# First block with a shared value tile, a late mirror and one home for the stage-1 table

## The chip, the cores and the metric

The kernel runs on one core of one Trainium2 chip. The metric is the device time of one launch in microseconds (us), taken as the median of three runs; less is better. TensorE is the matmul engine (PE in the profile, its weight loads PEld), DVE is VectorE, ACT is ScalarE, POOL is GpSimd, SP is SyncE, which here only issues DMAs.

## The reference

Two layers, one after the other. The first takes the real part of a two-dimensional Fourier transform of each batch, over 3008 rows and 256 columns. The second is a gated feed-forward layer on its result.

```python
X = np.fft.fft(np.fft.fft(x, axis=1), axis=2).real     # x: 8 x 3008 x 256, float32
t = X.reshape(24064, 256)
out = (np.maximum(t @ w_gate, 0) * (t @ w_val)) @ w_out  # w_gate, w_val: 256 x 1536, w_out: 1536 x 256
```

## The kernel before, in words

The row transform is factored as 94 x 32. Stage 1 (`stage1`, and `first_products` for batch 0) multiplies the input rows with a 94-point table of cosines and sines, a shuffle through memory turns the result, and stage 2 finishes the row transform with a small table `m2`. Its result per batch is three blocks of 512 columns, each held as a pair of bf16 tiles `pq` (pool `pqp`, five buffers). The column transform over 256 is not computed on the data: it is folded into the weights by `fold_w` with a table of cosines and sines, `cd` (the "D table"), at the start.

Because the input is real, each computed column gives two output rows, a direct one and a mirrored one. The feed-forward layer walks 288 steps t, 12 per block (`NF` = 12 slices of 128 of the hidden width). For a step, `gate(t)` (L615) puts the direct gate into one bank of PSUM, G, with two matmuls; ACT takes its relu as gs (L621); `mirror_gate(t)` (L623) adds a third matmul to the same G and ACT takes that relu as gm (L628). So the third matmul must wait until ACT has read G for gs. `value(t, 0)` and `value(t, 1)` (L630, matmul L634, weights wc and ws) put the direct value into V; `value(t, 2)` (weights wm) adds the mirror part on top. `direct_h` (L644) is a DVE product of gs and V, `mirror_h` (L650) of gm and the mirrored V. `out_piece` (L667) multiplies the products of the block before with `w_out`.

There are two forms of the loop. The first block (t = 0 to 11, loop at L790) has no output work yet. There the mirror value is made by the third matmul, which overwrites the direct value in place: `value(t, 2)` has to come after `direct_h(t)` has read V, and `mirror_h(t)` comes after it on DVE. A step writes, in the order of TensorE's queue: mirror gate of t-1, two gate matmuls of t, the mirror value of t-1, two value matmuls of t, then what `between(t)` hands in. From t = 12 on (loop at L804) the steps run in pairs, the mirror value is worked out on DVE and POOL (`even`, `mirror_value`), V of two steps is one tile of two banks, and out pieces are woven in.

The order of the work is written out by hand: every engine takes its instructions in the order of the program text, and a framework adds the semaphores that the tiles' reads and writes need. `between(t)` runs what the table `extra` holds for step t: in the first block the rest of the weight fold (`fold_w`, L329, two fp32 matmuls, an ACT copy and for the sine half a DVE product `scale_w`), of the stage between the two transforms (`upright`, `rotate`) and of stage 2; from t = 12 on, stage 1 of the next batch. `pace` hands POOL its share of folding the next batch's input.

`pair(t, name)` (L598) gives the tile that two steps t, t+1 share, each with its half. In the first block V is the exception: L601 to L605 give each step a whole two-bank tile of its own, of which it uses one half. The pool `psv` has two such buffers.

At the start (L348 to L570) ACT and DVE make the tables while the first batch arrives by DMA. `wn` (two signs of the stage-1 table) lies in the pool `sp`, which is given up after the start; `w1`, a copy of one half of it made by two ACT copies (L467, L530), stays for the later batches. The D table's three ACT instructions are L511 to L513. The read of `t1t` at L516 (`seen`) is a small DMA that SP issues when the ACT copy `first_evac(4)` (L515, code at L230) is done; eight weight loads and the first load of batch 1 stand behind it on SP.

Of the kernel before, what the change touches and what calls it, by code (L numbers as in the profile page):

```python
# [11 lines left out]
F32 = mybir.dt.float32  # L12
BF16 = mybir.dt.bfloat16
# [3 lines left out]
SB = bass.MemoryType.SB  # L17
# [27 lines left out]
def kernel(ctx: ExitStack, tc, x, w_gate, w_val, w_out, out):  # L45
# [3 lines left out]
    nc = tc.nc  # L49
    B, S, D = x.shape  # L50
    DF = w_gate.shape[1]
    NA, NB = 94, 32
    H = D // 2
    NF = DF // 128
# [5 lines left out]
    const = ctx.enter_context(tc.tile_pool(name="const", bufs=1, space=SB))  # L60
# [3 lines left out]
    psg = ctx.enter_context(tc.tile_pool(name="psg", bufs=2, space=PS))  # L64
    psv = ctx.enter_context(tc.tile_pool(name="psv", bufs=2, space=PS))
    pso = ctx.enter_context(tc.tile_pool(name="pso", bufs=1, space=PS))
    pqp = ctx.enter_context(tc.tile_pool(name="pqp", bufs=5, space=SB))

    ctx.enter_context(tc.manual_schedule())

# [64 lines left out]
                in_offset=bass.IndirectOffsetOnAxis(ap=ixf[:, k:k + 1], axis=0))  # L135

    turn = {"o": 0, "v": 0}

    def spare(name):

        turn["o"] += 1
        return pso.tile([128, 512], F32, tag=f"o{turn['o'] % 2}", name=name)

    def borrow(name):

        return pso.tile([128, 512], F32, tag=f"o{(turn['o'] + 1) % 2}", name=name)
# [8 lines left out]
    def stage1(b, c, evac):  # L155

        ps, eo = borrow("ps1"), xt[b]["eo"]
        for i in range(2):
            jj = 2 * c + i
            o = ps[0:96, i * D:(i + 1) * D]  # L160
            if jj:
                nc.tensor.matmul(o, lhsT=w1[:, jj, :], rhs=eo[:, jj, :], start=True, stop=True)  # L162
                continue
            for cs, lo, hi in ((0, 0, H + 1), (1, H + 1, D)):
                for k in range(2):
                    nc.tensor.matmul(ps[0:96, lo:hi], lhsT=wz[:, cs, k, :], rhs=eo[:, k * (J - 1), lo:hi],  # L166
                                     start=(k == 0), stop=(k == 1))
        evacuate(b, c, ps, evac)
# [9 lines left out]
        else:  # L178
            nc.vector.tensor_copy(dst, src)

    psf, tabs = {}, {}

    def ends(r, n):

# [99 lines left out]


    ix = const.tile([96, 2, B], I32, tag="ix")
    w1 = const.tile([NA, 16, 96], BF16, tag="w1")
    wz = const.tile([NA, 3, 2, 96], BF16, tag="wz")
    m2 = const.tile([128, 2, 128], BF16, tag="m2")
    rot = const.tile([128, 128], BF16, tag="rot")  # L290
# [13 lines left out]
    for n in range(DF // 512):  # L304
        for c in range(3):
            pair = hp.tile([128, 2, 512], F32, tag="h", name="wst")
            for i in range(2):
                wst[i, n, c] = pair[:, i, :]
    cd = hp.tile([128, 2, 512], F32, tag="h", name="cd")[:, :, 0:H]
# [38 lines left out]
    with tc.tile_pool(name="sp", bufs=1, space=SB) as sp:  # L348
        dve, pl = nc.vector, nc.gpsimd

        def residue(t, q, n, eng):

            eng.tensor_scalar(q, t, scalar1=1.0 / n, scalar2=RND, op0=ALU.mult, op1=ALU.add)
            eng.tensor_scalar(q, q, scalar1=-RND, scalar2=float(n), op0=ALU.add, op1=ALU.mult)
            eng.tensor_tensor(t, t, q, op=ALU.subtract)

        def sines(out, r, n, sign):
            nc.scalar.activation(out, r, ACTF.Sin, scale=sign * 2.0 * math.pi / n * (1.0 - 2e-7))

        def cosines(out, a, n):  # L360

            nc.scalar.activation(out, a, ACTF.Sin, scale=-2.0 * math.pi / n, bias=qpi[0:a.shape[0], :])

        def absolute(out, a):
            nc.scalar.activation(out, a, ACTF.Abs)
# [1 line left out]
        def iota(eng, out, pattern, base, mult):  # L367
            eng.iota(out, pattern=pattern, base=base, channel_multiplier=mult, allow_small_or_imprecise_dtypes=True)

        wn = tabs["wn"] = sp.tile([NA, 2, 16, 96], BF16, tag="wn", name="wn")  # L370
        tabs["wzn"] = sp.tile([NA, 2, 96], BF16, tag="wzn", name="wzn")
        tabs["back"] = sp.tile([NA, NB, H], BF16, tag="back", name="back")
        ixf = sp.tile([96, 3], I32, tag="ixf")
# [6 lines left out]
        da = sp.tile([128, H], F32, tag="da")  # L380
        dq = sp.tile([128, H], F32, tag="dq")
# [52 lines left out]
        def bits(shift, mask):  # L434
            ti = sp.tile([128, 1], I32, tag=f"b{shift}{mask}i")
            dve.tensor_scalar(ti[:], pi[:], scalar1=shift, scalar2=mask,
                              op0=ALU.logical_shift_right, op1=ALU.bitwise_and)
            tf = sp.tile([128, 1], F32, tag=f"b{shift}{mask}f")
            dve.tensor_copy(tf[:], ti[:])
            return tf  # L440
# [23 lines left out]
        for k in range(2):  # L464
            sines(free(wz[:], 192 * (k + 1), [97, 2], [2, 48]), both[0], S, 2.0 * k - 1.0)
        nc.scalar.mul(wn[:, 0, 9:16, :], wn[:, 1, 9:16, :], -1.0)
        nc.scalar.copy(w1[:, 1:10, :], wn[:, 1, 1:10, :])  # L467
        back(0, 2, "dve")
        dve.tensor_scalar(da[:], dd[:], scalar1=mi[:], scalar2=None, op0=ALU.mult)
        residue(da[:], dq[:], D, dve)  # L470
        jj, sl, up, odd = bits(0, 15), bits(4, 1), bits(5, 3), bits(0, 1)

        ends(24, 8)
# [34 lines left out]
        ends(16, 4)  # L508
        back(16, 4, "dve")
        dve.tensor_scalar(tis[:], tis[:], scalar1=NB - 1, scalar2=None, op0=ALU.bitwise_and)  # L510
        absolute(dq[:], da[:])  # L511
        cosines(cd[:, 0, 1:H], dq[:, 1:H], D)
        sines(cd[:, 1, 1:H], da[:, 1:H], D, 1.0)  # L513
        group((6, 7, 0), False)
        first_evac(4, "act")  # L515
        nc.sync.dma_start(out=seen[:], in_=t1t[0][0:1, 0, 8:10])  # L516
# [10 lines left out]
        first_evac(0, "dve")  # L527
        for cs in range(2):
            dve.tensor_tensor(m2[:, cs, :].rearrange("p (u k) -> p u k", u=4), sv[cs][:], ui[:], op=ALU.mult)
        nc.scalar.copy(w1[:, 10:16, :], wn[:, 1, 10:16, :])  # L530

        iota(pl, di[:], [[-32, 4], [-16, 2], [-1, 16]], 0, 1)
        pl.tensor_scalar(s2[:], mi[:], scalar1=1.0, scalar2=-2.0, op0=ALU.min, op1=ALU.mult)
# [60 lines left out]
    def split(t):  # L594

        return t >= NF

    def pair(t, name):  # L598

        e = pairs.setdefault(t // 2, {})  # L600
        if name == "V" and not split(t):  # L601
            name = f"V{t % 2}"
            if name not in e:
                e[name] = psv.tile([128, 2, 512], F32, tag="v", name="V")
            return e[name]  # L605
        if name not in e:
            pool, shape, dt = {"h": (hp, [128, 2, 2, 512], BF16), "gs": (gp, [128, 2, 512], F32),
                               "V": (psv, [128, 2, 512], F32), "gm": (ep, [128, 2, 512], F32),
                               "E": (ep, [128, 2, 512], F32)}[name]
            e[name] = pool.tile(shape, dt, tag=name.lower(), name=name)  # L610
        return e[name]
# [3 lines left out]
    def gate(t):  # L615
        b, blk, f = steps[t]
        pq, fs, ds = pqt[b, blk], slice(f * 128, (f + 1) * 128), direct(t)
        G = Gt[t] = psg.tile([128, 512], F32, tag="g", name="G")
        nc.tensor.matmul(G[:, ds], lhsT=wc[0][:, fs], rhs=pq[:, 0, ds], start=True, stop=False)  # L619
        nc.tensor.matmul(G[:, ds], lhsT=ws[0][:, fs], rhs=pq[:, 1, ds], start=False, stop=True)  # L620
        nc.scalar.activation(pair(t, "gs")[:, t % 2, ds], G[:, ds], ACTF.Relu)  # L621
# [8 lines left out]
    def value(t, k):  # L630
        b, blk, f = steps[t]
        cs = mirrored(t) if k == 2 else direct(t)
        w = (wc, ws, wm)[k][1]
        nc.tensor.matmul(pair(t, "V")[:, t % 2, cs], lhsT=w[:, f * 128:(f + 1) * 128],  # L634
                         rhs=pqt[b, blk][:, min(k, 1), cs], start=(k == 0), stop=(k > 0 or split(t)),
                         skip_group_check=(k == 2 or k == 1 and split(t)))
# [7 lines left out]
    def direct_h(t, n):  # L644

        ds, k = direct(t), slice(t % 2, t % 2 + n)
        nc.vector.tensor_tensor(pair(t, "h")[:, k, 0, 0:ds.stop - ds.start], pair(t, "gs")[:, k, ds],  # L647
                                pair(t, "V")[:, k, ds], op=ALU.mult)

    def mirror_h(t, n, eng, val):  # L650

        cols, k = mirrored(t), slice(t % 2, t % 2 + n)
        w = cols.stop - cols.start
        eng.tensor_tensor(free(pair(t, "h")[:], 1024 * (t % 2) + 512 + w - 1, [1024, n], [-1, w]),  # L654
                          pair(t, "gm")[:, k, cols], val[:, k, cols], op=ALU.mult)
# [89 lines left out]
    for n in (1, 2):  # L745
        t = 4 * n
# [36 lines left out]
    n = len(steps) // 2  # L783

    def between(t):
        for fn in extra.get(t, ()):
            fn()
        pace(t)

    for t in range(NF + 1):  # L790
        if t:
            mirror_gate(t - 1)
        if t < NF:
            gate(t)
        if t:
            value(t - 1, 2)
            mirror_h(t - 1, 1, nc.vector, pair(t - 1, "V"))
        if t < NF:
            value(t, 0)
            value(t, 1)  # L800
            direct_h(t, 1)
            between(t)

    for p in range(NF // 2, n + NF // 2):  # L804
        t = 2 * p
        live = p < n
        if NF // 2 < p <= n:
            mirror_gate(t - 1)
        if live:
            value(t, 0)  # L810
            value(t + 1, 0)
            gate(t)
        out_piece(t - NF, 0)
        between(t)
        if NF // 2 < p <= n:
            direct_h(t - 2, 2)
        if live:
            even(t)
            even(t + 1)
        out_piece(t - NF, 1)  # L820
        if live:
            mirror_gate(t)
            gate(t + 1)
        out_piece(t + 1 - NF, 0)
        between(t + 1)
        if NF // 2 < p <= n:
            mirror_value(p - 1)
        if live:
            value(t, 1)
            value(t + 1, 1)  # L830
        out_piece(t + 1 - NF, 1)
# [30 lines left out]
```

## Time and profile before

| what | value |
|---|---|
| median of 3 runs | 625.57 us (625.12 to 625.66) |
| the profiled execution's own time | 625.63 us |
| its span in the trace | 623.9 us |
| TensorE busy, share of the span | 612.0 us, 98% |
| DVE busy | 536.7 us, 86% |
| ACT busy | 445.5 us, 71% |
| POOL busy | 520.0 us, 83% |
| mean granted TensorE clock | 0.997 |

The profile describes one execution. Its times in us count from the start of the span, which is 1.7 us shorter than the time of that execution. A row of the timeline gives the start, the duration, the engine, the line, the operation with output and inputs, and in brackets how long the engine was idle ahead of it and who ended that. A matmul is shown from its start to the modelled end of its pipeline, so that matmuls in a dense stream overlap: with 496 columns one takes 0.37 us, and the next starts 0.21 us after it. Whether TensorE lost time is read from the distance between starts, not from the busy share.

### The profile page before, as it was taken

How to read it: one execution, taken by the hardware profiler on the slowest of the kernel's cores; microseconds unless marked ns; L12 is line 12 of the kernel's file. 1: busy time of each engine (PE TensorE's matmuls, PEld its weight loads, DVE VectorE, ACT ScalarE, POOL GpSimd, SP SyncE). 2: the span in 40 equal slices, each digit the busy share in tenths (PEclk: the TensorE clock that was granted, in tenths of full speed). 3: DMA queues.
4: the chain of work that ended last, by engine and by line, in shares of the span. 5: the costliest groups of instructions: out<-in, count | busy, mean ns of one | idle time of the engine just before them, and what ended most of it. 6: DMA issues, size and time to landing. Idle time of an engine off the chain costs nothing.

```text
span 623.9 us, 11929 instructions
## 1 busy us (share of the span) xinstructions
PE 612.0 (98%) x4252; PEld 409.3 (66%) x4284; DVE 536.7 (86%) x652; ACT 445.5 (71%) x857; POOL 520.0 (83%) x447
## 2 busy tenths in 40 slices
PE   8999999999999999999999999999999999999996
PEld 4345666766666666666667666666666666666665
DVE  7677898899889898888988998898988888899991
ACT  7676777777776767767677767767677776766660
POOL 8898898999888898899988998888988965565664
PEclk9999999999999999999999999999999999999998
DMA  8994282525553182613833255531822134112114
GB/s 168 240 169 109 82 219 67 134 65 163 125 136 79 34 234 71 164 36 86 222 100 92 63 162 127 134 82 34 230 72 61 34 85 125 52 34 67 34 35 99
DMA packets 42038, 67.44 MB, mean 108 GB/s; under 512 B 5877, under 2 KB 31774, under 8 KB 39962
## 3 DMA queue, kind: packets, MB, share of 16 engines
q1 hardware_dynamic: 37162, 50.61, 31.4%
q0 software_dynamic: 4656, 15.88, 10.7%
q8 instruction: 33, 0.54, 0.4%
q10 hardware_dynamic: 160, 0.20, 0.1%
q14 instruction: 27, 0.22, 0.1%
HBM read 38.85 MB, written 30.17 MB: 111 GB/s over the span
## 4 chain that ended last, share of the span: by engine, by line
PE 96%; DMA 1%; POOL 1%; issue 1%; DVE 1%; ACT 0%; POOLq 0%; DVEq 0%
PE po L683 40%; PE V L634 19%; PE G L619 10%; PE G L626 10%; PE G L620 10%; PE psw L333 2%; PE ps L162 2%; PE ps L271 2%; DMA lo<-in_x_dram 1%; POOL hi L132 0%; DVE h L647 0%; PE pst L240 0%; PE ps L216 0%; PE ps L166 0%; POOL lo L129 0%
## 5 line engine op out<-in xcount | busy, mean ns | idle before, releaser
L654 POOL TENSOR_TENSOR h<-gm,E 128x992 bf16<-128x992 f32 (+1 forms) x138 | 319.9, 2318 | 83.3 <-DVE E L661 54.4
L683 PE MATMUL po<-wo,h 128*128 128x256 bf16 (+2 forms) x2304 | 328.5, 272 | 0.4
L683 PEld LDWEIGHTS <-h 128*128 128x128 bf16 (+2 forms) x2304 | 231.4, 103 | 105.9
L628 ACT ACTIVATE gm<-G 128x496 f32<-128x496 f32 (+1 forms) x288 | 170.4, 592 | 94.7 <-PE G L626 87.7
L647 DVE TENSOR_TENSOR h<-gs,V 128x1024 bf16<-128x1024 f32 (+3 forms) x150 | 173.8, 1159 | 59.4 <-PE V L634 39.3
L641 DVE SCALAR_TENSOR_TENSOR E<-nb,af,V 128x496 f32<-128x496 bf16 (+1 forms) x276 | 190.2, 731 | 0.4 <-PE G L620 0.4
L621 ACT ACTIVATE gs<-G 128x497 f32<-128x497 f32 (+2 forms) x288 | 169.7, 589 | 25.3 <-PE G L620 25.2
L661 DVE SCALAR_TENSOR_TENSOR E<-E,V 128x992 f32<-128x992 f32 (+1 forms) x138 | 164.6, 1193 | 0.0
L619 PE MATMUL G<-pq,wc 128*128 128x496 bf16 (+2 forms) x287 | 107.6, 375 | 1.2
L620 PE MATMUL G<-pq,ws 128*128 128x497 bf16 (+2 forms) x288 | 108.0, 375 | 0.1
L626 PE MATMUL G<-pq,wm 128*128 128x496 bf16 (+1 forms) x288 | 107.9, 375 | 0.0
L634 PE MATMUL V<-pq,ws 128*128 128x496 bf16 (+2 forms) x280 | 83.7, 374 | 0.0
L634 PE MATMUL V<-pq,wc 128*128 128x496 bf16 (+2 forms) x266 | 80.7, 374 | 0.0
L620 PEld LDWEIGHTS <-ws 128*128 128x128 bf16 x288 | 28.2, 98 | 32.6
L696 ACT COPY os<-po 128x512 f32<-128x512 f32 x63 | 36.9, 586 | 14.3 <-PE po L683 11.7
L634 PEld LDWEIGHTS <-wc 128*128 128x128 bf16 x288 | 28.2, 98 | 20.7 <-issue 2.5
L114 POOL TENSOR_TENSOR eo<-xla 94x256 bf16<-94x256 f32 x56 | 40.5, 729 | 0.6
L619 PEld LDWEIGHTS <-wc 128*128 128x128 bf16 x288 | 28.2, 98 | 18.5 <-DVE pq L278 0.8
L114 POOL TENSOR_TENSOR eo<-xlb 94x256 bf16<-94x256 f32 (+1 forms) x42 | 34.4, 820 | 0.7
L111 POOL TENSOR_TENSOR xla<-xla,xha 94x510 f32<-94x510 f32 x28 | 32.9, 1175 | 2.2
L177 ACT CAST t<-ps 96x512 bf16<-96x512 f32 x56 | 32.7, 584 | 2.3 <-PE ps L162 0.2
L626 PEld LDWEIGHTS <-wm 128*128 128x128 bf16 x288 | 28.1, 98 | 4.4 <-issue 1.6
(142 smaller groups left out, 367.8 us busy)
## 6 DMA issues: line engine op xcount, KB each, us to landing
out_dram<-os SPq DMA_DIRECT2D x124, 128.0 KB
Td<-t SPq DMA_DIRECT2D x7, 768.0 KB
t<-Td SPq DMA_DIRECT2D x7, 768.0 KB
out_dram<-os SPq DMA_DIRECT2D x82, 64.0 KB
xla<-in_x_dram SPq DMA_DIRECT2D x7, 720.0 KB
xlb<-in_x_dram SPq DMA_DIRECT2D x6, 640.0 KB
nb<-Nd SPq DMA_DIRECT2D x23, 128.0 KB
out_dram<-os SPq DMA_DIRECT2D x40, 48.0 KB
```

The source lines that it names most:

```text
L114: yield eng.tensor_tensor(e1[:, :, k:k + H], x1[:, :, 0:H], free(x1, D, [DX, n], [-1, H]), op=op)
L619: nc.tensor.matmul(G[:, ds], lhsT=wc[0][:, fs], rhs=pq[:, 0, ds], start=True, stop=False)
L620: nc.tensor.matmul(G[:, ds], lhsT=ws[0][:, fs], rhs=pq[:, 1, ds], start=False, stop=True)
L621: nc.scalar.activation(pair(t, "gs")[:, t % 2, ds], G[:, ds], ACTF.Relu)
L626: nc.tensor.matmul(G[:, cols], lhsT=wm[0][:, f * 128:(f + 1) * 128], rhs=pqt[b, blk][:, 1, cols], start=False, stop=True, skip_group_check ...
L628: nc.scalar.activation(pair(t, "gm")[:, t % 2, cols], G[:, cols], ACTF.Relu)
L634: nc.tensor.matmul(pair(t, "V")[:, t % 2, cs], lhsT=w[:, f * 128:(f + 1) * 128], rhs=pqt[b, blk][:, min(k, 1), cs], start=(k == 0), stop=( ...
L641: nc.vector.scalar_tensor_tensor(pair(t, "E")[:, t % 2, cols], nbt[b, blk][:, cols], af[:, f:f + 1], pair(t, "V")[:, t % 2, cols], op0=ALU ...
L647: nc.vector.tensor_tensor(pair(t, "h")[:, k, 0, 0:ds.stop - ds.start], pair(t, "gs")[:, k, ds], pair(t, "V")[:, k, ds], op=ALU.mult)
L654: eng.tensor_tensor(free(pair(t, "h")[:], 1024 * (t % 2) + 512 + w - 1, [1024, n], [-1, w]), pair(t, "gm")[:, k, cols], val[:, k, cols], o ...
L661: nc.vector.scalar_tensor_tensor(E[:, :, cols], E[:, :, cols], 2.0, V[:, :, cols], op0=ALU.mult, op1=ALU.subtract)
L683: nc.tensor.matmul(po[0:m, i, :], lhsT=pair(t - f + ff, "h")[:, ff % 2, sg, g * 128:g * 128 + m], rhs=wo[:, ff, :], start=(ff == 0), stop= ...
```

## The change

In the first block V goes by `pair` like everything else: steps t and t+1 share one tile of two banks. The mirror value and its product move behind the direct work of the next step: the step now writes mirror gate of t-1, gate of t, value of t, `direct_h(t)`, then `value(t-1, 2)` and `mirror_h(t-1)`, then `between(t)`. The last mirror of the block goes into the first pair of the second loop, behind `gate(12)`. `wn` moves to the pool `const`, `w1` and its two copies go, and stage 1 of the later batches reads `wn`. One of the five buffers of `pqp` goes. The three ACT instructions of the D table move from behind `back(16, 4)` to right behind the DVE work that they read.

```diff
-    pqp = ctx.enter_context(tc.tile_pool(name="pqp", bufs=5, space=SB))
+    pqp = ctx.enter_context(tc.tile_pool(name="pqp", bufs=4, space=SB))
...
-                nc.tensor.matmul(o, lhsT=w1[:, jj, :], rhs=eo[:, jj, :], start=True, stop=True)
+                nc.tensor.matmul(o, lhsT=wn[:, 1, jj, :], rhs=eo[:, jj, :], start=True, stop=True)
...
-    w1 = const.tile([NA, 16, 96], BF16, tag="w1")
+    wn = tabs["wn"] = const.tile([NA, 2, 16, 96], BF16, tag="wn", name="wn")
...
-        wn = tabs["wn"] = sp.tile([NA, 2, 16, 96], BF16, tag="wn", name="wn")
...
         nc.scalar.mul(wn[:, 0, 9:16, :], wn[:, 1, 9:16, :], -1.0)
-        nc.scalar.copy(w1[:, 1:10, :], wn[:, 1, 1:10, :])
         back(0, 2, "dve")
         dve.tensor_scalar(da[:], dd[:], scalar1=mi[:], scalar2=None, op0=ALU.mult)
         residue(da[:], dq[:], D, dve)
+        absolute(dq[:], da[:])
+        cosines(cd[:, 0, 1:H], dq[:, 1:H], D)
+        sines(cd[:, 1, 1:H], da[:, 1:H], D, 1.0)
...
-        absolute(dq[:], da[:])
-        cosines(cd[:, 0, 1:H], dq[:, 1:H], D)
-        sines(cd[:, 1, 1:H], da[:, 1:H], D, 1.0)
         group((6, 7, 0), False)
         first_evac(4, "act")
...
-        nc.scalar.copy(w1[:, 10:16, :], wn[:, 1, 10:16, :])
...
         e = pairs.setdefault(t // 2, {})
-        if name == "V" and not split(t):
-            name = f"V{t % 2}"
-            if name not in e:
-                e[name] = psv.tile([128, 2, 512], F32, tag="v", name="V")
-            return e[name]
...
-    for t in range(NF + 1):
+    def last_value(t):
+
+        value(t, 2)
+        mirror_h(t, 1, nc.vector, pair(t, "V"))
+
+    for t in range(NF):
         if t:
             mirror_gate(t - 1)
-        if t < NF:
-            gate(t)
+        gate(t)
+        value(t, 0)
+        value(t, 1)
+        direct_h(t, 1)
         if t:
-            value(t - 1, 2)
-            mirror_h(t - 1, 1, nc.vector, pair(t - 1, "V"))
-        if t < NF:
-            value(t, 0)
-            value(t, 1)
-            direct_h(t, 1)
-            between(t)
+            last_value(t - 1)
+        between(t)
 
     for p in range(NF // 2, n + NF // 2):
         t = 2 * p
         live = p < n
-        if NF // 2 < p <= n:
+        if p <= n:
             mirror_gate(t - 1)
         if live:
             value(t, 0)
             value(t + 1, 0)
             gate(t)
+        if p == NF // 2:
+            last_value(t - 1)
```

More of the change, by code (lines that the diff above doesn't have):

```diff
@@ L137 @@
     turn = {"o": 0, "v": 0}
+    tabs = {}
     def spare(name):
@@ L179, in evacuate @@
             nc.vector.tensor_copy(dst, src)
-    psf, tabs = {}, {}
+    psf = {}
     def ends(r, n):
```

## The prediction, made before the result was known

> **What bounds the kernel now.** First the waits of TensorE, over the whole span (engine and line, whom it waited for: us in total, times, longest):
>
> ```profile
> PE V L634 <- DVE h L647: 1.4, 3, 0.8
> ...
> PE ps L216 <- ACT t L230: 0.4, 1, 0.4
> PE psw L333 <- DVE wm L327: 0.2, 1, 0.2
> ```
>
> TensorE is 98% busy; taking the distances between matmul starts against their dense spacing, I find no lost time after 51.4 us that isn't a missing record. So only a shift of the first 52 us can move the end, and whatever moves there moves it one for one. The waits on `direct_h` (L647) are the target of the late mirror, the wait at L216 that of the D table. Second, the timeline of TensorE at the end of the first block:
>
> ```profile
> 46.15 0.37 PE L626 MATMUL G<-pq,wm 128*128 128x496 bf16 x1
> ...
> 47.18 0.37 PE L634 MATMUL V<-pq,wm 128*128 128x496 bf16 x1 [0.24 <-DVE h L647]
> ...
> 48.96 0.37 PE L634 MATMUL V<-pq,wm 128*128 128x496 bf16 x1 [0.36 <-DVE h L647]
> ...
> 49.58 0.37 PE L626 MATMUL G<-pq,wm 128*128 128x496 bf16 x1
> 50.74 0.37 PE L634 MATMUL V<-pq,wm 128*128 128x496 bf16 x1 [0.79 <-DVE h L647]
> ```
>
> The mirror matmul (wm) of V comes late because it overwrites what `direct_h` reads. Six matmuls need 6 x 0.21 = 1.25 us; these steps take 1.5 to 1.8. Third, ACT and DVE there:
>
> ```profile
> 46.55 0.58 ACT L628 ACTIVATE gm<-G 128x496 f32<-128x496 f32 x1 [0.46 <-PE G L626]
> 47.03 0.58 ACT L621 ACTIVATE gs<-G 128x496 f32<-128x496 f32 x1
> ...
> 48.69 0.58 ACT L621 ACTIVATE gs<-G 128x496 f32<-128x496 f32 x1
> ```
>
> ```profile
> 48.24 0.66 DVE L647 TENSOR_TENSOR h<-gs,V 128x496 bf16<-128x496 f32 x1
> ```
>
> A mirror gate at time 0 gives gm at 0.41 and gs at 0.88 to 1.46, and the next mirror gate may start at 1.52: a loop through ACT that stays after the change. Also to be seen: gs of step 11 starts at 48.69 in one half of the tile whose other half the product that began at 48.24 still reads (0.66 us, to 48.90). Halves of an SBUF tile are kept apart. Fourth, the second loop, where V already is one tile of two steps:
>
> ```profile
> 108.44 0.58 PE L634 MATMUL V<-pq,wc 128*128 128x496 bf16 x2
> ...
> 109.19 1.37 DVE L641 SCALAR_TENSOR_TENSOR E<-nb,af,V 128x496 f32<-128x496 bf16 x2
> ```
>
> The two matmuls write the two halves and end at 108.81 and 109.02. The first `even` reads only the first half. Yet in the trace's semaphore records the first matmul raises no semaphore, the second does, and DVE's queue passes its wait for TensorE at 109.06, 0.04 after the second end. The same 0.04 comes back in many other pairs. In the other direction too: of two `even`s only the second raises a semaphore, and of the two wc/ws matmul pairs only the first waits. **In PSUM the halves of a V tile count as one tile.**
>
> **What the skill says.** "PSUM — Partial Sum Buffer", section "PSUM bank collisions raise a hardware error": two engines may use different banks at once. The trace agrees: at 45.87 to 46.54 `mirror_h` reads one V buffer while TensorE writes another from 45.81. So the chip asks for no wait between halves; it is the program's semaphores. "TensorE: Matmul & The Clock Gate", "Back-to-back issue gap": N/2.4 + 2.5 ns, 209 ns for 496 columns; the trace has 0.21. Its section "What's actually happening": the clock falls after an idle window of about 3.4 us. Gaps of 1.0 us in this trace left the granted clock at 0.997, and mine below are up to 1.4, so I add nothing. "ScalarE: Activation LUTs", "Table sets": functions of one set need no reload; the trace has one table load, though sines and copies alternate, so moving the D table adds none.
>
> **The change, part by part.**
>
> *The D table and the two copies.* ACT at 8.20 gets three instructions (0.93 us from first start to end at 13.34) where the first copy of `w1` (0.89) goes; ACT then idles until 9.80 (DMA), so nothing behind it moves. At 13.34 they go, and `first_evac(4)` starts when its matmuls end (13.79 + 0.04) instead of 14.18. TensorE, waiting at 14.71, starts 0.36 sooner. What is late next: the first `fold_w` at 16.62 needs the DVE difference L323, which waits for weights that land at 15.2, and ends at 16.63; its second half loads at 16.68 in either case. So at most 0.05 is left; I take 0. SP passes the wait at `seen` 0.36 sooner, with ten DMAs behind it; the DMA engines are idle from 15.2 to 16.8, so nothing is pushed aside. If that cover went, the gain would be 0.36. The second copy (0.67 at 17.14) ends as ACT's next input arrives: 0.
>
> *One home, four buffers.* Stage 1 reads equal values with equal loads: 0. A `pqp` buffer is written again four blocks on instead of five. Stage 2 of the next batch comes at steps 29 to 37 of a batch, and the block four places back was finished at steps 0, 12 and 24, at least 10 steps (some 20 us) before: 0. If wrong, a wait of a step, 2 us, per batch; I see no way to it.
>
> *The late mirror.* No instruction is added. `value(t-1, 2)` moves behind two value matmuls, its product behind `direct_h(t)`. Behind the waiting matmul stand all of `between(t)` and the next step, since TensorE works in order. Two cases by the parity of t:
>
> - t even: the mirror goes to the older pair, whose `direct_h` is long done. No wait; the old ones go.
> - t odd: t-1 and t share a tile. `direct_h(t)`, written just before, reads it. The mirror of t-1 writes the other half, and by the fourth view must wait for the end of `direct_h(t)`: that is for gs(t), 0.06 to the start, 0.67 for the product, 0.05 to TensorE.
>
> Price of the odd steps, from this trace: the slot of the moved matmul is where the sixth matmul of the step stands now, and gs(t) ends where it does now.
>
> | t | gs(t) ends | wait over at (+0.78) | slot | stall |
> |---|---|---|---|---|
> | 1 | 25.75 | 26.52 | 25.12 | 1.40 |
> | 3 | 30.80 | 31.57 | 30.38 | 1.19 |
> | 5 | 36.03 | 36.80 | 35.61 | 1.19 |
> | 7 | 41.49 | 42.26 | 41.07 | 1.19 |
>
> Together 4.97. TensorE is dense there except for 0.2 at 38.78, whose chain (fold, ACT, `scale_w`) moves along with it, so nothing is absorbed. Steps 9 to 12 (times without these 4.97): mirror gate at 44.62; gs(9) ends 46.10; mirror at 46.87; next mirror gate 47.08; even step 10 by the ACT loop 1.52, to 48.60; gs(11) ends 50.06, mirror at 50.84, mirror gate 51.05; two value and two gate matmuls, last mirror at 52.12, first out piece at 52.33. Before, it is at 51.81: +0.52. The even steps' mirror needs the product of the mirror before: done at 48.02 against a slot at 48.12 in step 10, 51.98 against 52.12 in step 12, so just no wait. DVE then has `even(13)` done 0.15 before its reader wants it.
>
> Sum: 4.97 + 0.52 - 0 = 5.5 us. From the first out piece on everything moves along: POOL's chain waits for DVE there (1.82 us idle at 57), so later input costs it nothing. On the profiled execution 625.63 + 5.5; on the median, 0.06 lower, **631.1**.
>
> The unknown is the tile rule. Bounds: each odd stall is 0 without it; with it, 1.2 to 1.4 plus up to 0.3 where the slack of 0.1 in an even step runs out. A shorter one is hard to get: gs cannot come sooner than the ACT loop lets it.
>
> **The rivals.**
>
> *B: the halves are kept apart, faster.* Place: the same matmul in odd steps. Then no stall, and steps 9 to 12 run on the ACT loop: mirror gates at 46.15, 47.66, 49.17, out piece at 50.45: 1.36 sooner, with up to 0.05 from the start. 625.57 - 1.4 = **624.2**. For it: SBUF halves are kept apart, and the chip allows it. Against: the fourth view. It decides when the mirror of t-1 may start before `direct_h(t)` has ended; below about 0.2 us of stall per odd step (6 x 0.2 = 1.2 against 1.4) the change wins.
>
> *C: only the bare steps lose.* If the waits under steps 1 to 7 lay beside the fold work that `between` hands in, +0.52 would be left: **626.1**. Against: `between` stands behind the moved matmul in TensorE's queue.
>
> **How the numbers follow.** A, the stalls: 0.84, own range 629.6 to 632.4 (one stall of 1.2 less, or 0.3 more in four even steps). B: 0.12. C: 0.04. A's range holds nearly all of A, about 0.8 in all. About 0.2% (1.25 us) is what a measurement here can tell from no change; B's 1.4 lies close to it, so I split B: 0.07 faster, 0.05 the same; of C, whose 0.5 lies below the bound, I give 0.03 to the same and 0.01 to slower. Faster 0.07, the same 0.08, slower 0.85.
>
> **What would show it.** In the profile after: mirror matmuls of V waiting on L647 in steps 1, 3, 5, 7, 9, 11, six times, 1.0 to 1.3 us each as listed, and none in even steps; the first out piece at about 57.3; nothing lost after it. For the D table: TensorE's wait at L216 down to about 0.1, but the upright matmuls still at 17.69. Wrong if the waits on L647 are gone and the out piece stands near 50.4 (B), or if PSUM semaphores are raised by each half alone.

## The result and the profile after

| | us |
|---|---|
| before, median of the runs beside it | 625.56 (625.12 to 625.66) |
| after, median | 630.50 (630.35 to 631.19) |
| ratio | 1.0082, 95% interval 1.0065 to 1.0100 |
| profiled execution after: own time, span | 630.35, 628.2 |

The changed kernel is slower by 4.94 us, 0.8%; the forecast was a rise of 5.5 us, to 631.1. In the changed kernel the lines have moved: the V matmul is L627 (L634 before), `direct_h` L640 (L647), `mirror_h` L647 (L654), the direct relu L614, the mirror gate L619, the out piece L676, the start's matmuls L217, the weights' sum and difference on DVE L322 and L324.

Part 1 of the page after, each engine's busy time:

```profile
PE 612.2 (97%) x4252; PEld 409.4 (65%) x4284; DVE 537.3 (86%) x652; ACT 444.1 (71%) x855; POOL 520.2 (83%) x447
```

No engine's busy time rose by more than 0.6 us. TensorE has its 612 us in a span that is 4.4 longer: the time is lost in waits. TensorE's waits, the profile's whole list (engine and line, whom it waited for: us in total, times, longest):

```profile
PE V L627 <- DVE h L640: 6.2, 6, 1.2
PE psk L398 <- DVE wk L392: 1.3, 1, 1.3
PE ps L217 <- DMA lo<-in_x_dram: 0.2, 1, 0.2
PE ps L217 <- ACT t L231: 0.2, 1, 0.2
PE psw L334 <- DVE wm L328: 0.2, 1, 0.2
PE ps L217 <- DVE hi L191: 0.2, 1, 0.2
```

The first line stands where 1.4 us, 3 times, stood: V now waits six times for the direct product, and 1.0 us each on average. (The wait at L398 is TensorE's first of all, up to 1.3 us of the span.) The timeline of TensorE in steps 9 to 12 shows two of the six:

```profile
49.63 0.37 PE L627 MATMUL V<-pq,ws 128*128 128x496 bf16 x1
50.98 0.37 PE L627 MATMUL V<-pq,wm 128*128 128x496 bf16 x1 [0.98 <-DVE h L640]
51.19 0.37 PE L619 MATMUL G<-pq,wm 128*128 128x496 bf16 x1
...
52.24 0.37 PE L627 MATMUL V<-pq,wm 128*128 128x496 bf16 x1
52.71 0.37 PE L619 MATMUL G<-pq,wm 128*128 128x496 bf16 x1
...
53.62 0.37 PE L627 MATMUL V<-pq,ws 128*128 128x496 bf16 x1
54.93 0.37 PE L627 MATMUL V<-pq,wm 128*128 128x496 bf16 x1 [0.94 <-DVE h L640]
...
56.21 0.37 PE L627 MATMUL V<-pq,wm 128*128 128x496 bf16 x1
56.42 0.38 PE L676 MATMUL po<-wo,h 128*128 128x256 bf16 x2
```

The mirror matmul (wm) that an odd step writes comes 1.35 or 1.31 after the matmul ahead of it instead of 0.21; the one that an even step writes (52.24, 56.21) has no wait. Next, what it waits for: ACT's direct relu of step 9, and DVE's two products behind that relu:

```profile
49.65 0.58 ACT L614 ACTIVATE gs<-G 128x496 f32<-128x496 f32 x1
```

```profile
50.26 0.67 DVE L640 TENSOR_TENSOR h<-gs,V 128x496 bf16<-128x496 f32 x1 [0.23 <-ACT gs L614]
51.39 0.67 DVE L647 TENSOR_TENSOR h<-gm,V 128x496 bf16<-128x496 f32 x1 [0.46 <-PE V L627]
```

The relu ends at 50.23, the direct product runs to 50.93, and TensorE writes the other half of the tile at 50.98, 0.05 later. DVE then idles 0.46 until that matmul is through.

For every trace I split the span at two marks: the first `upright` matmul (the first work after the start) and the first out piece. From the first out piece to the last it is 565.89 us in this kernel, the one before and all seven below, to 0.01. Thus every difference lies ahead of that loop, or in the end behind it.

| kernel | start to first upright | upright to out piece | behind the last out piece | span |
|---|---|---|---|---|
| before | 17.69 | 34.12 | 6.16 | 623.86 |
| after | 16.93 | 39.49 | 5.94 | 628.24 |
| e1_read_order | 17.19 | 33.06 | 6.10 | 622.24 |
| e2_own_tiles_late | 17.43 | 35.20 | 6.13 | 624.65 |
| e3_old_first_block | 17.34 | 34.09 | 5.98 | 623.31 |
| e4_shared_early | 16.77 | 39.89 | 5.98 | 628.52 |
| e5_pair_mirror | 17.69 | 32.99 | 6.11 | 622.68 |
| e6_no_weight_sum | 16.38 | 40.66 | 5.96 | 628.89 |
| e7_pair_mirror_end | 17.42 | 32.82 | 6.07 | 622.21 |

The second column, "the middle" below, is the first block. It is longer by 5.37 in the kernel after. The start doesn't follow the code: e4 has the start of the kernel before and comes to 16.77, e3 has the changed start and comes to 17.34. It follows the load of the first gate weights: DVE's sum of them waits for that load in all eight kernels that have the sum (all but e6). Here is the sum in the kernel before and in e4, whose starts have the same code:

```profile
15.21 0.69 DVE L321 TENSOR_TENSOR wst<-wst 128x512 f32<-128x512 f32 x1 [0.53 <-DMA wst<-in_moe_w_gate_dram]
```

```profile
14.29 0.69 DVE L321 TENSOR_TENSOR wst<-wst 128x512 f32<-128x512 f32 x1 [0.47 <-DMA wst<-in_moe_w_gate_dram]
```

In the eight kernels the sum starts between 14.29 and 15.21, and the first `upright` comes 2.48 after it each time. With the same code the start thus came out 0.92 apart in two profiled executions, so I judge an edit of the first block by its middle, and then by the ratio of the many runs.

### The profile page after: what moved, and what is told of

Same layout as the page of the kernel before. It is cut to its first block, busy times and chain, and to the rows that moved or that the text cites. A ratio compares the mean times of both kernels' runs of the same rounds, so it can differ in the third digit from the quotient of the medians.

```text
span 628.2 us, 11915 instructions
## 1 busy us (share of the span) xinstructions
PE 612.2 (97%) x4252; PEld 409.4 (65%) x4284; DVE 537.3 (86%) x652; ACT 444.1 (71%) x855; POOL 520.2 (83%) x447
## 4 chain that ended last, share of the span: by engine, by line
PE 94%; ACT 2%; DVE 1%; DMA 1%; issue 1%; POOL 1%; POOLq 0%
PE po L676 40%; PE V L627 18%; PE G L612 10%; PE G L619 10%; PE G L613 9%; PE psw L334 2%; PE ps L163 2%; PE ps L272 2%; DMA lo<-in_x_dram 1%; DVE h L640 1%; ACT gs L614 1%; ACT gm L621 1%; PE ps L217 0%; ACT wc L337 0%; PE ps L167 0%
## 5 line engine op out<-in xcount | busy, mean ns | idle before, releaser
L647 POOL TENSOR_TENSOR h<-gm,E 128x992 bf16<-128x992 f32 (+1 forms) x138 | 319.9, 2318 | 88.6 <-DVE E L654 57.7
L676 PE MATMUL po<-wo,h 128*128 128x256 bf16 (+2 forms) x2304 | 328.4, 272 | 0.4
L676 PEld LDWEIGHTS <-h 128*128 128x128 bf16 (+2 forms) x2304 | 231.4, 103 | 105.9
L640 DVE TENSOR_TENSOR h<-gs,V 128x1024 bf16<-128x1024 f32 (+3 forms) x150 | 173.9, 1159 | 65.8 <-PE V L627 41.1
L634 DVE SCALAR_TENSOR_TENSOR E<-nb,af,V 128x496 f32<-128x496 bf16 (+1 forms) x276 | 190.1, 730 | 0.0
L614 ACT ACTIVATE gs<-G 128x497 f32<-128x497 f32 (+2 forms) x288 | 169.7, 589 | 24.1 <-PE G L613 24.1
L654 DVE SCALAR_TENSOR_TENSOR E<-E,V 128x992 f32<-128x992 f32 (+1 forms) x138 | 164.3, 1191 | 0.0
L619 PE MATMUL G<-pq,wm 128*128 128x496 bf16 (+1 forms) x288 | 107.9, 375 | 0.1
L627 PE MATMUL V<-pq,ws 128*128 128x496 bf16 (+2 forms) x280 | 83.7, 374 | 0.0
L627 PE MATMUL V<-pq,wc 128*128 128x496 bf16 (+2 forms) x266 | 80.7, 374 | 0.0
L627 PEld LDWEIGHTS <-wc 128*128 128x128 bf16 x288 | 28.2, 98 | 18.7
L619 PEld LDWEIGHTS <-wm 128*128 128x128 bf16 x288 | 28.1, 98 | 6.7 <-issue 4.1
```

The costliest lines, as they stand in the source:

```text
L619: nc.tensor.matmul(G[:, cols], lhsT=wm[0][:, f * 128:(f + 1) * 128], rhs=pqt[b, blk][:, 1, cols], start=False, stop=True, skip_group_check ...
L634: nc.vector.scalar_tensor_tensor(pair(t, "E")[:, t % 2, cols], nbt[b, blk][:, cols], af[:, f:f + 1], pair(t, "V")[:, t % 2, cols], op0=ALU ...
L654: nc.vector.scalar_tensor_tensor(E[:, :, cols], E[:, :, cols], 2.0, V[:, :, cols], op0=ALU.mult, op1=ALU.subtract)
L676: nc.tensor.matmul(po[0:m, i, :], lhsT=pair(t - f + ff, "h")[:, ff % 2, sg, g * 128:g * 128 + m], rhs=wo[:, ff, :], start=(ff == 0), stop= ...
```

## The experiments

Two theories stood against each other. **Tile rule:** for the program's semaphores the two halves of the shared V count as one, so that the late mirror value, written behind `direct_h` of the same tile in the program, waits for it. **Chip:** TensorE can't write one bank of the pair while DVE reads the other, or the product is simply late wherever it stands. The text above each "Measured" was written before that kernel ran. Where an edit adds or takes away lines of the program, the line numbers of its profile are shifted, so they are named there.

**e1_read_order: the same instructions, another order in the text.** The late mirror value is written ahead of the direct product instead of behind it. On every engine the instructions stand in the same order as in the kernel after; only which access of the tile is recorded first, and so which semaphores are waited for, is another.

```diff
-        direct_h(t, 1)
         if t:
-            last_value(t - 1)
+            value(t - 1, 2)
+        direct_h(t, 1)
+        if t:
+            mirror_h(t - 1, 1, nc.vector, pair(t - 1, "V"))
         between(t)
```

> The kernel after, with one line moved: the mirror value matmul of step t-1 is written ahead of the direct product of step t instead of behind it. Each engine still gets the same instructions in the same order; only what waits for what can change. Theory A (the halves of a V tile count as one tile, so the matmul waits for a product that it has nothing to do with): the six waits on the direct product go, the first block runs on the ACT loop of 1.52 us in its last steps, and the time is 624.2 us, 1.4 below the kernel before. Rival (the late order itself costs: ACT and DVE hold TensorE up in the odd steps whatever the semaphores): no change, 630.5 us.

Measured: 624.18 us (623.65 to 624.69), before beside it 625.05; ratio 0.9986, interval 0.9979 to 0.9993. TensorE's waits in e1, the whole list:

```profile
PE psk L398 <- DVE wk L392: 1.3, 1, 1.3
PE psw L334 <- DVE wm L328: 0.2, 1, 0.2
```

The six waits for L640 are gone. In step 1, where the changed kernel lost 1.39, the timeline of e1 has the three V matmuls in a row, 0.21 apart, and the direct product after them:

```profile
24.17 0.37 PE L627 MATMUL V<-pq,wc 128*128 128x496 bf16 x1
24.38 0.37 PE L627 MATMUL V<-pq,ws 128*128 128x496 bf16 x1
24.59 0.37 PE L627 MATMUL V<-pq,wm 128*128 128x496 bf16 x1
```

```profile
25.25 0.67 DVE L640 TENSOR_TENSOR h<-gs,V 128x496 bf16<-128x496 f32 x1 [1.73 <-ACT gs L614]
```

So the late place of the mirror is no loss in itself, the program's order of reading and writing the tile is. The chip theory falls by the same step, here in the kernel after:

```profile
25.00 0.67 DVE L640 TENSOR_TENSOR h<-gs,V 128x496 bf16<-128x496 f32 x1 [1.73 <-ACT gs L614]
```

```profile
25.72 0.37 PE L627 MATMUL V<-pq,wm 128*128 128x496 bf16 x1 [1.23 <-DVE h L640]
```

The mirror matmul is 1.39 late, so TensorE had stood since 24.33, 0.67 before there was any read to collide with. What e1 does not show is whether the chip would bear the two accesses at once: here the read comes later. Its gain in the middle is 1.06, where the prediction's rival B has 1.36 for a kernel without the rule. The even steps still meet the rule, now against the mirror product of the same tile (e5 and e7 below take that away). TensorE and DVE in step 10 of e1:

```profile
46.45 0.37 PE L627 MATMUL V<-pq,ws 128*128 128x496 bf16 x1
46.96 0.37 PE L627 MATMUL V<-pq,wm 128*128 128x496 bf16 x1
```

```profile
46.25 0.66 DVE L647 TENSOR_TENSOR h<-gm,V 128x496 bf16<-128x496 f32 x1
```

The wm matmul starts 0.05 after the end of the product, 46.91, and 0.30 late; in step 12 it is 0.29 late. (Between the modelled end of the matmul ahead of it and its start only 0.14 are idle, and the list of waits above has no gap as short as that.)

**e2_own_tiles_late: late mirror, own tiles.** The lines that gave each step of the first block a V tile of its own are put back into the changed kernel; the mirror stays late.

```diff
+        if name == "V" and not split(t):
+            name = f"V{t % 2}"
+            if name not in e:
+                e[name] = psv.tile([128, 2, 512], F32, tag="v", name="V")
+            return e[name]
```

> The kernel after, but each step of the first block has a V tile of its own again; the late mirror stays. Theory A: the waits on the direct product go. In their place the direct value of t waits for a free tile, which the mirror product of t-2 gives; with fold work between the steps this is hidden, in steps 9 to 12 it costs about 0.7 us each, so the time is about 626.5 us. Rival (the late order costs): near 630.5 us, with the waits still at the mirror value matmul.

Measured: 626.40 (625.91 to 626.94), ratio 1.0021, interval 1.0014 to 1.0028; the middle is 1.08 longer than before. One of its waits, and one place of it on TensorE (in this kernel L632 is the V matmul, L652 the mirror product):

```profile
PE V L632 <- DVE h L652: 2.6, 4, 1.0
```

```profile
49.57 0.37 PE L632 MATMUL V<-pq,wc 128*128 128x496 bf16 x1 [0.58 <-DVE h L652]
```

With own tiles the waits for the direct product are gone, but a new one takes their place: there are two buffers, the mirror product of t-2 gives one up a step later, and the first value matmul of t stands until it has. The two halves of the change, this one and the sharing alone in e4, are thus each a loss alone, by other waits. e2 also rules out that a write of V simply waits for whatever DVE work stands last ahead of it in the text: the order of the text is that of the changed kernel, only the tiles differ, and the mirror value doesn't wait. A first block with V in tiles of one bank each was not tried.

**e4_shared_early: shared tiles, early mirror.** The other half alone: the kernel before without the five lines of e2.

> The kernel before, with the V tile shared by two steps and nothing else: the mirror stays early. Theory A: in odd steps the direct value matmul, which writes the other half, now waits for the mirror product written just before it; the mirror value's slot plus 0.37 for it, 0.05, 0.67 for the product and 0.05 make a stall of 1.0 to 1.1 us in each of six odd steps, 631.5 us in all. Rival (halves are kept apart, and the late order is what costs): 625.6 us.

Measured: 630.43 (630.29 to 630.93), ratio 1.0089, interval 1.0073 to 1.0104; the middle is 5.77 longer. TensorE's waits on V (L629 is the V matmul here, L649 the mirror product, L642 the direct one):

```profile
PE V L629 <- DVE h L649: 5.1, 6, 1.0
PE V L629 <- DVE h L642: 1.2, 3, 0.6
```

```profile
43.32 0.67 DVE L649 TENSOR_TENSOR h<-gm,V 128x496 bf16<-128x496 f32 x1 [0.21 <-PE V L629]
...
44.04 0.37 PE L629 MATMUL V<-pq,wc 128*128 128x496 bf16 x1 [0.83 <-DVE h L649]
```

The direct value of an odd step, which goes into the empty half, waits for the mirror product that reads the full one, to 0.05 after its end. So with the early mirror, too, sharing a tile costs much. My 6.0 was 0.2 above the middle. The median lies 1.07 below the 631.5. Of that, 0.23 is the middle, and 0.51 comes from the base: the kernel before has a median of 625.05 in the 47 runs beside this one and 625.56 in the four beside the result. The rest isn't accounted for.

**e3_old_first_block: everything but the first block.** The changed kernel with the loop and tiles of before; one home for `wn`, no copies, four `pqp` buffers and the early D table stay.

```diff
+        if name == "V" and not split(t):
+            name = f"V{t % 2}"
...
-    for t in range(NF):
+    for t in range(NF + 1):
...
-        direct_h(t, 1)
...
         if t:
-            last_value(t - 1)
-        between(t)
+            value(t - 1, 2)
+            mirror_h(t - 1, 1, nc.vector, pair(t - 1, "V"))
+        if t < NF:
+            value(t, 0)
+            value(t, 1)
+            direct_h(t, 1)
+            between(t)
...
```

> The kernel after, with the first block of the kernel before (own V tiles, early mirror): only the table's home, the two copies, the four buffers and the earlier D table are left of the change. Theory A: TensorE's wait at the first products of c = 0 shrinks by 0.36 us, and the weights' difference on DVE takes the gain back: 625.5 us, the same as before. Rival (the gain arrives whole, and the 0.5 us by which the change lost less than was summed comes from here): 625.0 to 625.2 us.

Measured: 625.05 (624.49 to 625.37) beside 625.05; ratio 0.9998, interval 0.9989 to 1.0006. The middle is 34.09 against 34.12. The 625.05 itself lies in the rival's range, but the kernel before moved there too, and the interval, about 0.7 us less to 0.4 more, doesn't exclude a gain of 0.36. The trace does, if the weights' difference on DVE is what the first fold waits for. From the timeline of e3:

```profile
14.87 0.69 DVE L322 TENSOR_TENSOR wst<-wst 128x512 f32<-128x512 f32 x1 [0.63 <-DMA wst<-in_moe_w_gate_dram]
...
15.60 0.69 DVE L324 TENSOR_TENSOR wst<-wst 128x512 f32<-128x512 f32 x1
...
16.34 0.19 PEld L334 LDWEIGHTS psw<-wst,cd 128*64 128x64 f32 x2 [0.53 <-DVE wst L324]
...
17.34 0.45 PE L241 MATMUL pst<-perm,t 128*128 128x128 bf16 x5
```

DVE waits for the weights' DMA, the fold's weight load waits for DVE (its end, 16.29), and `upright` comes 1.06 after that end. The same 1.06 stands between the two in the kernel before (16.63 and 17.69), after (15.87 and 16.93), e1, e2 and e4. An earlier D table can't move `upright` as long as the load and DVE's sum and difference end later.

**e6_no_weight_sum: the cover of the D table taken away.** The sum and difference of the first weight block are left out of the changed kernel, so that its first fold has no DVE work to wait for.

```diff
-        for k, w in ((0, wst[i, n, 2]), (1, wst[i, n, 0])):
+        for k, w in ((0, wst[i, n, 2 if n or i else 1]), (1, wst[i, n, 0])):
...
-        pair_w(0, 0, dve)
```

> The kernel after, with the sum and the difference of the first 512 gate weight columns left out (the fold takes the raw halves), so that the first fold waits for the landed weights alone; its values are not those of the layer. Theory A (the weights' difference on DVE takes the earlier D table's gain back): the first upright matmul, which starts 1.06 us behind the end of that difference in all six kernels seen so far, now starts 1.06 us behind the first fold matmul, 2.97 us behind the first matmul of c = 0 instead of 3.10. Rival (something else is late, as the products' copies): 3.1 us or more.

Measured, one execution: 631.02. From the first column product of the start (the matmul that the D table lets start sooner) to `upright` it is 2.92 us; before it is 2.97, after 3.10, in e1 3.47 and in e3 3.75. So of the kernels with the early D table this one has the shortest stretch, 0.18 below the kernel after, which agrees with that pair being what was late next. (In the kernel before the products themselves end no sooner than the pair, at 16.70 and 16.63.) But the total doesn't gain, since the next fold has its own cover. POOL's difference of the next weights and TensorE in e6:

```profile
18.15 1.26 POOL L324 TENSOR_TENSOR wst<-wst 128x512 f32<-128x512 f32 x1
...
18.38 2.17 PE L334 MATMUL psw<-wst,cd 128*64 128x512 f32 x4
...
19.47 0.19 PEld L334 LDWEIGHTS psw<-wst,cd 128*64 128x64 f32 x2 [0.90 <-POOL wst L324]
```

What the upright gains, 0.55 against the kernel after, comes back as a wait of 0.90 here, and the middle is 1.17 longer. Not all of this is the cover: POOL's difference ends at 19.42, in the kernel after at 18.78, because POOL's sum ahead of it started 0.24 later and took 1.81 instead of 1.27; why isn't known. But in the kernel after the same weight load also goes right behind that difference, at 18.84, so an earlier `upright` would have had to wait there in any case. It was one execution and is compared by its trace alone.

**e5_pair_mirror: both mirror products of a tile at once.** If the even steps of e1 wait for the mirror product of the same tile, there should be no such product between the two mirror values. e5 writes the mirror values like e1, and makes the two products of a tile as one DVE instruction of 992 columns in the even step after them.

```diff
...
-        direct_h(t, 1)
         if t:
-            last_value(t - 1)
+            value(t - 1, 2)
+        direct_h(t, 1)
+        if t and t % 2 == 0:
+            mirror_h(t - 2, 2, nc.vector, pair(t - 2, "V"))
         between(t)
...
         if p == NF // 2:
-            last_value(t - 1)
+            value(t - 1, 2)
...
             even(t + 1)
+        if p == NF // 2:
+            mirror_h(t - 2, 2, nc.vector, pair(t - 2, "V"))
```

> The kernel after, with the mirror value matmul written ahead of the direct product in every step, and the mirror products of two steps made by one DVE instruction in the even step, behind the second mirror value (for the last pair behind the two evens of the next block). Theory A: what is left of the tile rule in the read-order kernel, 0.30 us in each of steps 10 and 12 where the mirror value waits for the mirror product of the step before, goes as well. From the first upright matmul to the first out piece 32.8 us instead of 33.07, against 34.1 in the kernel before; the time 1.4 us below the kernel before, about 623.7 us. Rival (the ACT loop, not the tile rule, holds those steps): 33.1 us, and the time of the read-order kernel, about 624.2.

Measured: 624.15 (623.47 to 625.32) beside 624.90, ratio 0.9987, interval 0.9980 to 0.9994. The middle is 32.99, 0.07 better than e1 where 0.26 was expected, and the time is the one named for the rival. The two waits of 0.30 are gone all the same; a new one has come, seen on DVE and TensorE in e5:

```profile
34.44 1.18 DVE L647 TENSOR_TENSOR h<-gm,V 128x992 bf16<-128x992 f32 x1
...
35.54 0.68 DVE L247 CAST t<-pst 128x512 bf16<-128x512 f32 x1
...
36.27 0.20 PEld L334 LDWEIGHTS psw<-wst,cd 128*64 128x64 f32 x4 [0.27 <-DVE t L247]
```

The long product delays the copy behind it in DVE's queue (in e1 that copy starts at 34.51), and TensorE waits for that copy.

**e7_pair_mirror_end: the double product only where nothing stands behind it.** In steps 1 to 8 the mirror products stay single as in e1; the double form is for the products of steps 8 to 11, when the fold work is over. The rest of the edit is that of e5.

```diff
...
+        if 0 < t < NF - 3:
+            mirror_h(t - 1, 1, nc.vector, pair(t - 1, "V"))
+        elif t == NF - 2:
+            mirror_h(t - 2, 2, nc.vector, pair(t - 2, "V"))
...
```

> The pair-mirror kernel, with the pair form kept for the last two pairs of the first block alone (steps 8 to 11); in steps 1 to 8 the mirror products are single, as in the read-order kernel. In the pair-mirror kernel the DVE product of 1.18 us stood ahead of a PSUM copy that the fold of step 5 waits for, 0.16 us at 36.28. Theory A: that wait goes, the waits of the read-order kernel at steps 10 and 12 stay away, and from the first upright matmul to the first out piece it takes 32.8 us (32.99 there, 33.07 in the read-order kernel, 34.12 in the kernel before); the time 1.1 to 1.3 us below the kernel before. Rival (what those two kernels lack is the ACT loop's): 33.0 us and 0.8 to 0.9 below the kernel before.

Measured: 623.93 (623.23 to 624.62) beside 624.86, ratio 0.9981, interval 0.9975 to 0.9988. The middle is 32.82, 1.30 below before, as expected. The time fell by 0.93, less than the 1.1 to 1.3 expected; the 0.37 between the two isn't explained. The last steps of e7 on ACT:

```profile
46.26 0.58 ACT L621 ACTIVATE gm<-G 128x496 f32<-128x496 f32 x1 [0.46 <-PE G L619]
46.74 0.58 ACT L614 ACTIVATE gs<-G 128x496 f32<-128x496 f32 x1
47.78 0.58 ACT L621 ACTIVATE gm<-G 128x496 f32<-128x496 f32 x1 [0.46 <-PE G L619]
48.26 0.58 ACT L614 ACTIVATE gs<-G 128x496 f32<-128x496 f32 x1
49.30 0.58 ACT L621 ACTIVATE gm<-G 128x496 f32<-128x496 f32 x1 [0.46 <-PE G L619]
```

A step is 1.52 from one gm to the next, and the 0.46 waits are for the mirror gate: this is the loop through ACT, and it is all that is left there. e7 has the shortest middle and the lowest median of the nine kernels, below the kernel before by 0.19% and below the change by about 6.6 us; the intervals of e1, e5 and e7 overlap, so that it beats those two is seen in the middle alone.

## Why the prediction was right

- **Bound, and "whatever moves there moves the end one for one".** Right: the loop of out pieces takes 565.89 in every kernel, with first blocks from 32.8 to 40.7 us long.
- **Halves of a V tile count as one.** Right, and shown by e1 and e4: with the record order alone turned, the six waits vanish; with the sharing alone, the middle grows by 5.77. In e2, with own tiles and the order kept, the waits for the direct product are gone as well.
- **The table of stalls.** Lost between starts: 1.39, 1.18, 1.18 and 1.18 in steps 1, 3, 5 and 7, against 1.40 and 1.19. Steps 9 and 11 lose 1.14 and 1.10. None in an even step.
- **Steps 9 to 12, +0.52.** The changed kernel loses 2.51 there (1.14, 0.26 for the ACT loop, 1.10); before, the five gaps from 45.40 to 50.74 come to 2.15. That is +0.36. Together with 4.93 for the four early stalls it makes 5.29 of the 5.37 measured; this term of the sum was too large by 0.16. The rest lies in two gaps of less than 0.1.
- **D table, copies, home and buffers at nothing.** Right: e3's ratio is 0.9998, with an interval too wide to exclude 0.36 by itself. TensorE's wait at L217 for ACT fell from 0.4 to 0.2 (forecast 0.1), and the upright matmul stayed tied to DVE's difference, 1.06 behind it, in every kernel that has one. One reading beside it was off: the DMA engines were busy 11% to 16% of the time from 15.2 to 15.8, and idle only after that; nothing hangs on it.
- **"Upright still at 17.69", and the out piece at 57.3.** They came at 16.93 and 56.42, 0.76 and 0.9 sooner. In that execution DVE's difference ended 0.76 sooner, and DVE had waited for the weights' load; e4 shows as early a start with the old code, e5 one at 17.69 with the new. So the early start isn't due to the change. Why these loads land earlier in some executions was not tried. Start and end differ by up to 1 us between executions, which is enough for the 0.43 between 5.37 in the middle and 4.94 in the medians; that they make up just this 0.43 isn't shown. Against 625.05, the median of the 47 runs of the kernel before beside e1 to e4, the rise would be 5.45, but the changed kernel wasn't run beside those.
- **Rival B** priced the change without the rule at -1.36. e1 got 1.06, e7 1.30 in the middle: the price was right, but the changed code didn't reach it. **Rival C**, stalls hidden beside fold work, is refuted: all four arrive whole.
- **The clock.** The page "TensorE: Matmul & The Clock Gate" of the Trainium skill, section "What's actually happening", has the clock fall after an idle window of about 3.4 us. The stalls, up to 1.39 us and each 4 to 7 us behind the one before, left the granted clock at 1.00 from 17 to 57 us. It falls, to 0.50, only behind the last matmul of the launch: 2.1 us after that in e5, which is sooner than the page's figure, and 5.3 us after it in e7. What the mean granted clock of 0.998 lacks to 1 is this end.
- **The range.** Its lower end, 629.6, is 0.3 below what its own reason (one stall of 1.2 less) gives.

## What to carry to other kernels

When two steps share a tile of PSUM, ask in which order the program text records the accesses of its two halves: here a write recorded behind a slow reader of the other half waited for it, though every engine's own queue was unchanged, and turning two lines of text was worth 6.4 us of the first block. Before you combine two instructions into a longer one, ask whether another engine waits for what stands behind it in its queue; in e5 that left 0.07 us of a gain that is 0.24 in e7. And when a tuned start is moved, look first for what is late next; here 0.36 us on ACT was worth nothing since a load and two DVE instructions came later anyway.

## What the runs showed that I had not expected

- The start to the first `upright` matmul lies between 16.8 and 17.7 us over the eight profiled executions with the weights' sum, and goes with the landing of the weights and not with the code. That spread is as large as the 0.9 that e1 or e7 gain, so in this kernel a gain under 1 us is seen only in many runs (21 each) or in the middle of the trace.
- Turning the record order doesn't only repair the change, it makes late mirroring a gain: 0.14% below before (interval 0.07% to 0.21%).
- A DVE product of 992 columns from PSUM takes 1.18 us and two of 496 take 0.67 and 0.66, with the second starting 0.59 after the first (25.25 and 25.84 in e1), 1.25 together. One instruction thus saves 0.07 of DVE's time, at the end of the pair. What e7 gains over e1, 0.24 in the middle, goes with the two waits of 0.30 that are gone.
